# Relaying the opening of a fused QK-norm attention and leaky-ReLU MLP kernel on one core

## The chip, the cores and the metric

The kernel runs on one core of a Trainium2 chip. A core has four compute engines, each with a queue of its own that it works through in order: TensorE (PE, matmuls and transposes), VectorE (DVE), ScalarE (ACT) and GpSimd (POOL). SyncE (SP) issues most of the transfers; POOL and ACT can issue some too. Engines wait for each other only through semaphores. The metric is the device time in microseconds of one execution.

## The reference

```python
def _attn_ref(q, k, v, g_q, g_k):          # q, k, v: 8 x 12 x 448 x 64
    def rmsnorm(x, g):
        rms = np.sqrt(np.mean(x * x, axis=-1, keepdims=True) + 1e-06)
        return x / rms * g
    q_n, k_n = (rmsnorm(q, g_q), rmsnorm(k, g_k))
    scores = 1.0 / np.sqrt(64) * np.matmul(q_n, k_n.transpose(0, 1, 3, 2))
    attn = np.exp(scores - np.max(scores, axis=-1, keepdims=True))
    attn = attn / (np.sum(attn, axis=-1, keepdims=True) + 1e-09)
    return np.matmul(attn, v)

# x: the heads side by side, 3584 tokens x 768
h = x @ w_in                               # 768 x 2048
out = np.maximum(0.01 * h, h) @ w_out      # 2048 x 768
```

## The kernel before

**Units.** The attention is worked through in 24 units: one batch and four of its twelve heads each (NQ = 3 units to a batch). A unit goes through these steps, each in a function of its own:

- `load` (L104) brings q and k of the unit with two transfers on SP into the tiles rq and rk (three buffers each); `load_v` (L110) brings v on POOL's queue into one of four tiles.
- The squares of q and k: `prep_sq` (L129) on ACT or `prep_sqp` (L133) on POOL. Their sums along each row, `prep_ssq` (L140), on DVE. One over the root, `prep_rinv` (L145), on ACT, as the exponential of minus half a logarithm. The product of the data with it, `prep_norm` (L150), on DVE: this is called norm(u) here. It reads two tensors in SBUF. The squares on POOL read two as well.
- The transposes: on PE in units 0 to 5 (`prep_tr`, L158, with a copy out of PSUM by DVE or ACT), by a transfer (`prep_trd`, L165) later.
- `qk` (L185) computes the scores transposed, seven steps t of 128 keys by 448 queries for four heads, into one of two PSUM slots. `ex` (L192) exponentiates a step on ACT, with a shift that is the same for the whole unit. The shift comes from the maximum of step 0: `shift_max` (L208, DVE) reduces along the rows and builds a diagonal, `shift_mm` (L226) spreads it over the partitions by a matmul with ones on PE and takes the maximum on DVE. For units 1 and 2, `score0` (L203) computes step 0 into two banks outside the slots.
- `zsum_slot` (L255) or `zcol` (L261) sums the exponentials by matmuls with ones, `pv` (L319) multiplies with v, `zinv` (L308) inverts the sums on ACT, `xmul` (L329) multiplies, which gives three pieces of x per batch.

**The two matmuls of the MLP** are cut into items of about a microsecond of PE time, which wait in a list (`queue`, filled by `push`, L499, when a batch is complete). `fill` (L534) runs after each quarter d of a unit and takes as many items from the list as its rate asks for; between the items it emits jobs of the coming units (`jobs`: norms, sums of squares, loads). The second matmul of two row blocks at a time is done with seven products in place of eight (`seven`, L422), with sums of blocks of the weights (`weight_sum`, L398, into the tile tw) and of the activations (s1 to s4, into the tile sa). The evacuations of the banks ma, mb, mc and md by DVE or ACT are not emitted at once, but put on a list (`pend`, through `later`, L419), which the next item empties (`flush`, L372) before its own matmuls. At the end of `fill`, L552 empties that list, and then L553 emits the jobs that are left over.

**The opening** is written out by hand (L576 to L746). Units 0, 1 and 2 are prepared there, and PE is given filler matmuls (`warm`, L572) in places where it would have nothing to do. `gate(u)` (L242) copies a single element of norm(u) on POOL, so that whatever comes after it in POOL's queue waits until that norm is done. The squares of units 1 to 8 are on POOL. `close(u)` (L642) ends unit u: sums, the first two exponentials of the next unit around them, products, and the inverse. The order in which the functions are called is the order in each engine's queue.

The weights come through POOL's queue: `load_w_in` (L87) in two halves of four transfers, `load_w_out` (L92) in two transfers.

The four names that the prediction uses most: rinv is the result of `prep_rinv`; sq are the squares; dg the diagonal; eb the finished shift.

Of the kernel before, what the change touches and what calls it, by code (L numbers as in the profile page):

```python
# [18 lines left out]
def kernel(  # L19
# [11 lines left out]
    nc = tc.nc  # L31
# [23 lines left out]
    def aux(shape, dtype, name):  # L55
        return psum.tile(shape, dtype, tag="aux", bufs=4, name=name)
# [53 lines left out]
    def load_v(u):  # L110
        nc.gpsimd.dma_start(vts[u % NV].rearrange("p a t d -> p a (t d)"), rows(v, u))  # L111
# [21 lines left out]
    def prep_sqp(u, tis=BOTH):  # L133
        for ti in tis:
            nc.gpsimd.tensor_tensor(buf(u, f"sq{ti}"), raw[u][ti], raw[u][ti], op=ALU.mult)
# [236 lines left out]
    def flush():  # L372
        while pend:
            pend.pop(0)()
# [159 lines left out]
    def fill(u, d, jobs):  # L534
        total = sum(c for c, _ in queue)
        left = WD[d] + 3.0
        uu, dd = u, d
        while True:
            dd += 1
            if dd == 4:  # L540
                uu, dd = uu + 1, 0
            if uu == NU or (fed(uu, dd) and (u > 3 or uu > 3)):
                break
            left += WD[dd]
        debt[0] += total * WD[d] / left
        while queue and debt[0] >= queue[0][0] * 0.5:
            c, fn = queue.pop(0)
            fn()
            debt[0] -= c
            if jobs:  # L550
                jobs.pop(0)()
        flush()  # L552
        for job in jobs:  # L553
            job()

    def vcopy(dst, src, scaled=False):
        if scaled:
# [18 lines left out]
    with tc.manual_schedule():  # L576
# [19 lines left out]
        nc.vector.tensor_copy(gcol, gps[:, 0:1])  # L596
        prep_ssq(0, ALL, (1,))
        prep_rinv(0, (1,))
        prep_sqp(1, (0,))
        load_v(0)  # L600
        load_v(1)
        prep_norm(0, CA, (0,))
        prep_norm(0, CB, (0,))
        prep_tr(0, 0, ((CA, acopy), (CB, acopy)))
        prep_norm(0, K0, (1,))
        tpk = aux([P, NS, P], FP16, "tp")

        def trk(c, copy):
            for x in range(*c):
                nc.tensor.transpose(tpk[:, x, :], buf(0, "n16")[:, 1, x].rearrange("p a d -> p (a d)"), ident16)  # L610
            copy(buf(0, "qkT")[:, 1, c[0]:c[1]], tpk[:, c[0]:c[1]])

        trk(K0, vcopy)
        prep_norm(0, K1, (1,))
        qk(0, STEPS[0])
        shift_max(0)
        trk(K1, acopy)
        load(3)
        prep_sqp(1, (1,))
        gate(0)  # L620
        load_w_in(0, 1024)
        prep_sqp(2)
        shift_bank(0)
        warm(12, st[0]["pb"])
        shift_mm(0)
        load_v(2)
        prep_ssq(1, ALL, (0,))

        def feed(u):
            load(u + 4)  # L630
# [8 lines left out]
            zsum(u, t0, t1)  # L639
            pv(u, t0, t1)  # L640

        def close(u):  # L642
            n = u + 1
            zsum_slot(u)
            ex(n)
            qk(n, (1,))
            pv(u)
            zinv(u)

        ex(0)  # L650
        prep_ssq(1, ALL, (1,))
        prep_rinv(1)
        prep_norm(1)
        prep_ssq(2)
        feed(0)
        load_w_in(1024, 1024)
        wb = aux([P, 512], FP32, "warm")
        qk(0, (1,))
        ex(0)
        warm(16, wb)  # L660
        qk(0, (2,))
        ex(0)
        warm(12, wb)
        qk(0, (3,))
        ex(0)
        warm(6, wb)
        qk(0, (4,))
        ex(0)
        trn(1, 0, vcopy)
        trn(1, 1, acopy)  # L670
        qk(0, (5,))
        ex(0)
        qk(0, (6,))
        ex(0)
        prep_rinv(2)
        score0(1)
        shift_max(1)
        shift_bank(1)
        warm(20, st[1]["pb"])
        shift_mm(1)  # L680
        close(0)

        prep_norm(2)
        prep_ssq(3)
        ex(1)
        feed(1)
        for f in range(2):
            load_w_out(8 * f, 8)
# [8 lines left out]
        ex(1)  # L697
        qk(1, (5,))
        ex(1)
        prep_rinv(3)  # L700
        score0(2)
        shift_max(2)
        qk(1, (6,))
# [1 line left out]
        shift_bank(2)  # L705
        warm(12, st[2]["pb"])
        shift_mm(2)
        close(1)

        prep_norm(3)  # L710
        ex(2)
        feed(2)
        qk(2, (2,))
        ex(2)
# [33 lines left out]
        for u in range(3, NU):  # L748
            for d in range(4):
                if d > 0 or u > 3:  # L750
                    qk(u, STEPS[d])
                    if d == 0:
                        shift_max(u)
                        if narrow(u - 1):
                            pv_slot(u - 1)
                            zcol(u - 1)
                            shift_mm(u)
                            pv_out(u - 1)
                            zcol_sum(u - 1)
                        else:  # L760
                            zsum_slot(u - 1)
                            pv(u - 1)
                            shift_mm(u)
                            zinv(u - 1)
                    ex(u)
                jobs = []

                def job(fn, *args):
                    jobs.append(lambda: fn(*args))

                if d == 0:
                    if u == 3:
                        prep_norm(4)
                        gate(4)
                    elif narrow(u - 1):
                        job(zcol_inv, u - 1)
                    else:
                        xmul(u - 1)
                    if u + 4 < NU:
                        job(load, u + 4)  # L780
                    if u + 3 < NU:
                        load_v(u + 3)
                    if u < 6:
                        prep_sqp(u + 3)
                if d == 1 and narrow(u - 1) and not 5 <= u < 8:
                    xmul_pool(u - 1)
                if fed(u, d) and u > 3:
                    push(u // NQ - 1)
                if (u, d) in ((3, 1), (4, 0)):
                    for ti in range(2):  # L790
                        prep_tr(u + 1, ti, VV)
                if d == 1 and 5 <= u < NU - 1:
                    job(prep_g, u + 1)
                if u + 2 < NU:
                    if d == 1:
                        for ti in range(2):
                            job(prep_ssq, u + 2, ALL, (ti,))
                    if d == 2:
                        job(prep_rinv, u + 2)
                        for ti in range(2):  # L800
                            job(prep_norm, u + 2, ALL, (ti,))
                        if u > 3:
                            job(prep_trd, u + 2)
                if d == 1 and 4 <= u < 8:
                    job(weight_sum, u - 4, 0)
                if d == 0 and 5 <= u < 9:
                    job(weight_sum, u - 5, 1)
                if d == 2 and 5 <= u < 8:
                    job(xmul_sb, u - 1)
                if d == 3 and 6 <= u < NU - 3:  # L810
                    for ti in range(2):
                        job(prep_sq, u + 3, ALL, (ti,))
                fill(u, d, jobs)
# [36 lines left out]
```

## Time and profile before

| | |
|---|---|
| median of 4 runs | 431.1 us (430.36 to 431.43) |
| the profiled execution | 431.01 us, span 429.2 us |
| PE busy | 409.5 us (95%) |
| ACT busy | 306.4 us (71%) |
| DVE busy | 270.9 us (63%) |
| POOL busy | 87.2 us (20%) |
| mean granted TensorE clock | 0.987 |
| first sum or product of the MLP on PE | 46.47 us |

The span is from the first to the last instruction of the profiled execution; its own time is 1.8 us longer. A share of busy time over the whole span is an average over stages with different limits, so the table of busy times by stage says more. In the timelines each line has the start, the time that the group of instructions covers, the engine, the line of the kernel, the operation and the tiles (result, arrow, sources), the shape, the count, and in brackets the idle time before it with what ended it. Ends of neighbouring instructions overlap by about 0.1 us, since the next begins while the last drains.

### The profile page before, as it was taken

What the parts mean: (1) busy time and instruction counts of PE and PEld (TensorE: products, weight loads), DVE (VectorE), ACT (ScalarE), POOL (GpSimd) and SP (SyncE); (2) the same over time, 40 slices, a digit from 0 to 9 for tenths busy, and PEclk for the clock granted to TensorE, in tenths of its full rate; (3) what the DMA queues carried; (4) which work ended last, traced back from release to release, by engine and by line L of the source; (5) the groups of instructions that cost most, each with busy time, mean ns of one, the idle gap of its engine ahead of it and who ended that gap; (6) DMA issues with size and microseconds to landing.
All of it is one profiled execution on the core that took longest, in us unless ns stands there. A gap on an engine that the chain in (4) does not pass through costs nothing.

```text
span 429.2 us, 8844 instructions
## 1 busy us (share of the span) xinstructions
PE 409.5 (95%) x3645; PEld 211.0 (49%) x3645; DVE 270.9 (63%) x434; ACT 306.4 (71%) x466; POOL 87.2 (20%) x77
## 2 busy tenths in 40 slices
PE   7687999999999999999999999999999999999996
PEld 6454444444444544455445544455445544455563
DVE  5887656888669865487359864587449840541162
ACT  5569888757986779967986789967986767643400
POOL 2985323300002102111102102111101101110000
PEclk9869999999999999999999999999999999999999
DMA  7999992789656896578665797478672460212013
GB/s 265 219 243 248 240 270 52 121 182 221 168 105 116 190 214 159 143 135 193 170 111 130 190 192 171 130 141 188 169 110 44 118 150 10 44 38 73 2 45 103
DMA packets 66476, 62.37 MB, mean 145 GB/s; under 512 B 35716, under 2 KB 61572, under 8 KB 66436
## 3 DMA queue, kind: packets, MB, share of 16 engines
q1 hardware_dynamic: 55840, 49.62, 46.4%
q0 software_dynamic: 10272, 11.80, 18.0%
q8 instruction: 28, 0.46, 0.4%
q10 hardware_dynamic: 324, 0.39, 0.3%
q14 instruction: 12, 0.10, 0.1%
HBM read 45.61 MB, written 11.01 MB: 132 GB/s over the span
## 4 chain that ended last, share of the span: by engine, by line
PE 66%; ACT 18%; DVE 9%; issue 2%; DMA 1%; SPq 0%; ACTq 0%; DVEq 0%
PE hps L347 23%; ACT et L201 9%; PE md L427 7%; PE mc L427 7%; PE sT L182 6%; PE ma L427 6%; PE sT L326 5%; ACT gt L341 4%; PE op L387 3%; DVE n L154 3%; PE zc L269 3%; PE mb L427 2%; ACT x L281 1%; PE sT L252 1%; ACT zs L292 1%
## 5 line engine op out<-in xcount | busy, mean ns | idle before, releaser
L201 ACT ACTIVATE et<-sT,eb 128x896 f16<-128x896 f32 x166 | 158.3, 1003 | 15.7 <-PE sT L182 13.3
L347 PE MATMUL hps<-xt,win 128*128 128x448 f16 x756 | 151.1, 353 | 0.2 <-DVE xt L335 0.2
L347 PEld LDWEIGHTS <-win 128*128 128x128 f16 x756 | 70.6, 98 | 71.5 <-issue 10.2
L341 ACT ACTIVATE gt<-hps 128x448 f16<-128x448 f32 x126 | 65.6, 540 | 19.4 <-PE hps L347 18.7
L306 POOL TENSOR_TENSOR xt<-x,rz 128x896 f16<-128x896 f32 x16 | 33.5, 2092 | 149.6 <-DMA rz<-zs 57.0
L154 DVE TENSOR_TENSOR n<-rq,rinv 128x896 f16<-128x896 f32 (+2 forms) x25 | 28.5, 1142 | 47.5 <-ACT rinv L148 44.1
L182 PE MATMUL sT<-qkT 64*64 64x448 f16 x664 | 52.5, 367 | 5.6 <-ACT et L201 4.8
L142 DVE TENSOR_REDUCE ssq<-sq 128x14 f32<-128x896 f32 (+2 forms) x49 | 50.3, 1057 | 0.7 <-ACT sq L131 0.7
L427 PEld LDWEIGHTS <-sa 128*128 128x128 f16 x352 | 32.8, 98 | 26.3 <-issue 6.1
L281 ACT COPY x<-sT 128x896 f32<-128x896 f32 x19 | 17.2, 906 | 37.8 <-DVE sT L232 37.8
L111 POOL DMA_DIRECT2D vt<-in_v_dram x24 | 18.2, 758 | 112.6 <-PE sT L326 105.1
L219 DVE TENSOR_REDUCE sT<-sT 128x1 f32<-128x896 f32 x22 | 24.1, 1094 | 18.1 <-PE sT L182 18.1
L182 PEld LDWEIGHTS <-qkT 64*64 64x64 f16 x672 | 15.8, 105 | 39.6 <-issue 36.1
L427 PEld LDWEIGHTS <-gt 128*128 128x128 f16 x264 | 25.2, 98 | 19.0 <-issue 2.9
L387 PE MATMUL op<-wout,gt 128*128 128x384 f16 x192 | 34.1, 327 | 0.0
L427 PE MATMUL ma<-wout,gt 128*128 128x384 f16 x176 | 32.2, 326 | 0.4
L326 PE MATMUL sT<-et,vt 64*64 64x448 f16 x532 | 28.5, 349 | 0.3
L154 DVE TENSOR_TENSOR n<-rk,rinv 128x896 f16<-128x896 f32 (+2 forms) x25 | 28.2, 1128 | 0.0
L408 DVE TENSOR_TENSOR sa<-gt 128x512 f16<-128x512 f16 (+1 forms) x15 | 8.1, 542 | 30.3 <-ACT gt L341 30.3
L326 PEld LDWEIGHTS <-vt 64*64 64x64 f16 x672 | 20.4, 107 | 10.9 <-issue 1.1
L387 PEld LDWEIGHTS <-gt 128*128 128x128 f16 x192 | 17.7, 98 | 14.0 <-issue 3.2
L453 ACT COPY ost<-ma 128x384 f32<-128x384 f32 x11 | 5.3, 478 | 23.7 <-PE ma L427 23.7
(87 smaller groups left out, 444.6 us busy)
## 6 DMA issues: line engine op xcount, KB each, us to landing
rq<-in_q_dram SPq DMA_DIRECT2D x24, 448.0 KB, 5.0
rk<-in_k_dram SPq DMA_DIRECT2D x24, 448.0 KB, 5.9
out_dram<-ost SPq DMA_DIRECT2D x52, 192.0 KB, 4.1
rz<-zs SPq DMA_DIRECT2D x38, 224.0 KB, 3.3
vt<-in_v_dram POOLq DMA_DIRECT2D x24, 224.0 KB, 5.1
win<-in_moe_w_in_dram POOLq DMA_DIRECT2D x8, 384.0 KB, 8.6
wout<-in_moe_w_out_dram POOLq DMA_DIRECT2D x2, 1536.0 KB, 22.7
out_dram<-ost SPq DMA_DIRECT2D x4, 96.0 KB, 2.1
```

Source lines behind the costliest of these rows:

```text
L142: nc.vector.tensor_reduce(buf(u, "ssq")[:, ti, :, c[0]:c[1]], buf(u, f"sq{ti}")[:, :, c[0]:c[1]], axis=AXL.X, op=ALU.add)
L154: nc.vector.tensor_tensor(buf(u, "n16")[:, ti, c[0]:c[1]].rearrange("p s a d -> p a s d"), src[:, :, c[0]:c[1]], buf(u, "rinv")[:, ti, :, ...
L182: nc.tensor.matmul(banks[a][64 * r:64 * r + 64, 0:S].rearrange("p (t x) -> p t x", t=NS), kT(u, r, a, t), qT(u, r, a), start=True, stop=True)
L201: nc.scalar.activation(s["et"][:, t], sT[:, :, 0:S], AF.Exp, bias=s["eb"], scale=1.0)
L219: nc.vector.tensor_reduce(s["spare"][:, 511:512], sT[:, :, 0:S], axis=AXL.XY, op=ALU.max)
L281: nc.scalar.copy(s["x32"], s["pslot"][:, :, 0:S])
L306: eng.tensor_tensor(xts[b][:, g], s["x32"], s["rz"], op=ALU.mult)
L326: nc.tensor.matmul(s["pv"][r][64 * a:64 * a + 64, 0:S], vts[u % NV][64 * r:64 * r + 64, a, t], s["et"][64 * r:64 * r + 64, t, a], start=(t ...
L341: nc.scalar.activation(dst, src, AF.Prelu, bias=0.0, scale=1.0, alpha=0.01)
L347: nc.tensor.matmul(hps[:, 0:S], win16[:, kt // 2, kt % 2, ts(ft, P)], xt[:, kt // 2, kt % 2], start=(kt == 0), stop=(kt == KT - 1))
L387: nc.tensor.matmul(op2[:, 0:HC], gt[:, ft, ds(col(t), P)], wout16[:, ft, ds(HC * half, HC)], start=(ft == 0), stop=(ft == FT - 1))
L427: nc.tensor.matmul(bank[:, 0:HC], a[:, f], b[:, f], start=(first and f == 0), stop=(f == HF - 1), skip_group_check=not first)
```

## The change

The opening is written in another order, and two things in the loop are moved.

- POOL's queue now begins with `gate(0)`. After it come the v of unit 0, the squares of unit 2, the first half of w_in, the v of units 1 and 2, `gate(1)`, the second half of w_in, and the squares of unit 3. The squares of unit 1 are computed on ACT instead, between the copies of unit 0's transposes.
- The transposes of unit 0 are done by a function `tr`, which takes a PSUM tile of its own for each chunk of q. Norm K1 is emitted before K0's copy.
- Unit 1's rinv is computed in two parts among the exponentials of unit 0; its norm in three pieces; its transposes, scores of step 0 and maximum follow after the fifth exponential of unit 0, and the matmul that finishes its shift after the last one. The copies of its transposes go to ACT (q) and DVE (k).
- `close` is dissolved: after the shift of unit u + 1 come the sums of squares of unit u + 2, two exponentials of unit u + 1, then the sums and the products of unit u, the rinv of unit u + 2, the inverse of unit u, and norm(u + 2). This is done at the end of units 0 and 1.
- The fillers between the exponentials change in number and place (6 before the matmul of the shift of unit 0 instead of 12, then 12 and 16 instead of 16, 12, 6 and 20).
- In `fill`, the left-over jobs are emitted first, and then the pending evacuations.
- The second half of each weight sum is emitted in the last quarter of the same unit, instead of the first quarter of the next.

```diff
@@ -549,9 +549,9 @@
             debt[0] -= c
             if jobs:
                 jobs.pop(0)()
-        flush()
         for job in jobs:
             job()
+        flush()
 
     def vcopy(dst, src, scaled=False):
         if scaled:
@@ -596,35 +596,39 @@
         nc.vector.tensor_copy(gcol, gps[:, 0:1])
         prep_ssq(0, ALL, (1,))
         prep_rinv(0, (1,))
-        prep_sqp(1, (0,))
-        load_v(0)
-        load_v(1)
         prep_norm(0, CA, (0,))
         prep_norm(0, CB, (0,))
-        prep_tr(0, 0, ((CA, acopy), (CB, acopy)))
         prep_norm(0, K0, (1,))
-        tpk = aux([P, NS, P], FP16, "tp")
-
-        def trk(c, copy):
-            for x in range(*c):
-                nc.tensor.transpose(tpk[:, x, :], buf(0, "n16")[:, 1, x].rearrange("p a d -> p (a d)"), ident16)
-            copy(buf(0, "qkT")[:, 1, c[0]:c[1]], tpk[:, c[0]:c[1]])
-
-        trk(K0, vcopy)
         prep_norm(0, K1, (1,))
+
+        def tr(u, ti, chunks, tp=None):
+            if tp is None:
+                tp = aux([P, NS, P], FP16, "tp")
+            for c, copy in chunks:
+                for x in range(*c):
+                    nc.tensor.transpose(tp[:, x, :], buf(u, "n16")[:, ti, x].rearrange("p a d -> p (a d)"), ident16)
+                copy(buf(u, "qkT")[:, ti, c[0]:c[1]], tp[:, c[0]:c[1]], ti == 0)
+            return tp
+
+        tr(0, 0, ((CA, acopy),))
+        tr(0, 0, ((CB, acopy),))
+        tpk = tr(0, 1, ((K0, vcopy),))
+        prep_sq(1, ALL, (0,))
         qk(0, STEPS[0])
         shift_max(0)
-        trk(K1, acopy)
+        tr(0, 1, ((K1, acopy),), tpk)
+        prep_sq(1, ALL, (1,))
         load(3)
-        prep_sqp(1, (1,))
         gate(0)
+        load_v(0)
+        prep_sqp(2)
         load_w_in(0, 1024)
-        prep_sqp(2)
+        load_v(1)
+        load_v(2)
         shift_bank(0)
-        warm(12, st[0]["pb"])
+        warm(6, st[0]["pb"])
         shift_mm(0)
-        load_v(2)
-        prep_ssq(1, ALL, (0,))
+        prep_ssq(1)
 
         def feed(u):
             load(u + 4)
@@ -639,50 +643,48 @@
             zsum(u, t0, t1)
             pv(u, t0, t1)
 
-        def close(u):
-            n = u + 1
-            zsum_slot(u)
-            ex(n)
-            qk(n, (1,))
-            pv(u)
-            zinv(u)
-
         ex(0)
-        prep_ssq(1, ALL, (1,))
-        prep_rinv(1)
-        prep_norm(1)
-        prep_ssq(2)
-        feed(0)
-        load_w_in(1024, 1024)
-        wb = aux([P, 512], FP32, "warm")
+        prep_rinv(1, (0,))
         qk(0, (1,))
         ex(0)
-        warm(16, wb)
+        prep_rinv(1, (1,))
+        prep_norm(1, ALL, (0,))
+        prep_norm(1, K0, (1,))
+        prep_norm(1, K1, (1,))
+        load(4)
+        gate(1)
+        load_w_in(1024, 1024)
+        prep_sqp(3)
+        load_v(3)
+        wb = aux([P, 512], FP32, "warm")
+        warm(12, wb)
         qk(0, (2,))
         ex(0)
-        warm(12, wb)
+        warm(16, wb)
         qk(0, (3,))
+        tr(1, 0, ((ALL, acopy),))
+        tpk = tr(1, 1, ((K0, vcopy),))
         ex(0)
-        warm(6, wb)
         qk(0, (4,))
         ex(0)
-        trn(1, 0, vcopy)
-        trn(1, 1, acopy)
+        tr(1, 1, ((K1, vcopy),), tpk)
+        score0(1)
+        shift_max(1)
         qk(0, (5,))
         ex(0)
         qk(0, (6,))
         ex(0)
+        shift_bank(1)
+        shift_mm(1)
+        prep_ssq(2)
+        ex(1)
+        qk(1, (1,))
+        ex(1)
+        zsum_slot(0)
+        pv(0)
         prep_rinv(2)
-        score0(1)
-        shift_max(1)
-        shift_bank(1)
-        warm(20, st[1]["pb"])
-        shift_mm(1)
-        close(0)
-
+        zinv(0)
         prep_norm(2)
-        prep_ssq(3)
-        ex(1)
         feed(1)
         for f in range(2):
             load_w_out(8 * f, 8)
@@ -697,7 +699,6 @@
         ex(1)
         qk(1, (5,))
         ex(1)
-        prep_rinv(3)
         score0(2)
         shift_max(2)
         qk(1, (6,))
@@ -705,10 +706,16 @@
         shift_bank(2)
         warm(12, st[2]["pb"])
         shift_mm(2)
-        close(1)
+        prep_ssq(3)
+        ex(2)
+        qk(2, (1,))
+        ex(2)
+        zsum_slot(1)
+        pv(1)
+        prep_rinv(3)
+        zinv(1)
 
         prep_norm(3)
-        ex(2)
         feed(2)
         qk(2, (2,))
         ex(2)
@@ -801,10 +808,8 @@
                             job(prep_norm, u + 2, ALL, (ti,))
                         if u > 3:
                             job(prep_trd, u + 2)
-                if d == 1 and 4 <= u < 8:
-                    job(weight_sum, u - 4, 0)
-                if d == 0 and 5 <= u < 9:
-                    job(weight_sum, u - 5, 1)
+                if d in (1, 3) and 4 <= u < 8:
+                    job(weight_sum, u - 4, d // 2)
                 if d == 2 and 5 <= u < 8:
                     job(xmul_sb, u - 1)
                 if d == 3 and 6 <= u < NU - 3:
```

## The prediction

> **What bounds the kernel now.** I read the stage table first: busy time per engine in four stretches, then the granted TensorE clock, the DMA share and GB/s.
>
> ```profile
> core 0: us, PE busy (x) PEld busy (x) DVE busy (x) ACT busy (x) POOL busy (x), PEclk, DMA share, GB/s
> 15.00:30.00 15.00, 10.79 (x133) 6.94 (x134) 12.84 (x15) 9.05 (x15) 13.11 (x16) 0.77 1.13 231
> 30.00:46.50 16.50, 13.13 (x226) 7.94 (x219) 13.34 (x21) 16.24 (x23) 9.97 (x10) 1.00 1.12 247
> 46.50:100.00 53.50, 50.68 (x474) 24.81 (x470) 40.03 (x57) 40.49 (x62) 13.29 (x11) 1.00 0.81 169
> 100.00:388.00 288.00, 286.64 (x2503) 140.93 (x2496) 183.28 (x295) 223.72 (x339) 44.01 (x30) 1.00 0.62 137
> ```
>
> From 46.5 us on TensorE is full (286.64 of 288.00), so the end moves one for one with two things: when that stretch starts, and any new PE wait in it. From 30 to 46.5 ScalarE is full (16.24 of 16.50): the exponentials set the pace. Before 30 neither is; DVE and POOL are (12.84 and 13.11 of 15.00). The list of waits says how little PE waits after 100 us:
>
> ```profile
> PE sT L231 <- DVE dg L221: 0.7, 3, 0.2
> ```
>
> The timelines of POOL and DVE (start, duration) show what fills 16 to 22:
>
> ```profile
> 16.40 1.69 POOL L135 TENSOR_TENSOR sq<-rq 128x896 f32<-128x896 f32 x1
> ...
> 16.67 2.38 DVE L154 TENSOR_TENSOR n<-rq,rinv 128x896 f16<-128x896 f32 x1 [0.70 <-issue]
> ...
> 18.04 2.54 POOL L135 TENSOR_TENSOR sq<-rk 128x896 f32<-128x896 f32 x1
> ...
> 18.98 2.56 DVE L154 TENSOR_TENSOR n<-rk,rinv 128x896 f16<-128x896 f32 x1
> ...
> 27.59 1.09 DVE L154 TENSOR_TENSOR n<-rq,rinv 128x896 f16<-128x896 f32 x1
> ```
>
> A norm takes 1.09 alone. Beside a square on POOL the two take turns: norm q ends 1.0 after the first square, the second square ends 1.6 after norm q, norm k 1.0 after that. So norm(1) ends at 21.54 instead of about 18.7. The transposes of unit 1 and ScalarE (idle 2.18 at 20.2 and 2.21 at 25.5) wait for it.
>
> **The opening, part by part.** I walk the new order with the old durations; ex(u,t) is exponential t of unit u (0.91 start to start).
>
> 1. Shift of unit 0. Norm K1, blocked 9.80 to 11.35 by POOL's square of unit 1, now runs 8.6 to 9.5; K0's copy ends 9.62; CB's transposes no longer wait for CA's copy, so scores start at 9.75 (was 10.23). Maximum 1.08, diagonal 0.29, matmul 0.23, 0.30 and 0.16: shift ready at 12.6 (was 13.98; six fewer fillers stand before the matmul). The two squares of unit 1 on ScalarE (0.95 each, k data landed 9.97) fit behind the copies, done 12.4. Gain 1.35.
> 2. Norm(1). Sums of squares to 13.65 and 14.6, rinv q to 14.2, ex(0,1), rinv k to 15.5; norm q 14.6 to 15.65, K0, K1 to 16.75. POOL is then issuing w_in, which the norms are priced as not disturbing: at 27.1 and 27.7 the same issues ran beside a norm of 1.09 and took 0.63 to 0.68. Was 21.54. The split rinv costs 0.52 more of ScalarE.
> 3. Shift of unit 1. q copy on ScalarE 16.35 to 17.35, K1 copy on DVE to 17.9, scores 0.4, two maxima 1.16, then 1.3 to the shift: 20.9, just as ex(0,6) ends (12.6 + 7 x 0.91 + two rinv 1.07 + copy 1.0 = 21.0). So ex(1,0) starts at 21.0, was 27.73. The sums and products of unit 0 move behind ex(1,1); their 28 matmuls of sums (1.5) are done at 22.5 and ScalarE wants them at 23.6, so the move is free unless PE is over 1 us late.
> 4. Norm(2) wants 23.6 (two sums of squares after the shift, rinv after ex(1,1)). What is late next is POOL. Its queue: gate(0) 9.6, v0, squares(2) 11.1 to 14.45 (data landed 11.08 and 12.27), w_in 4 x 0.63 to 17.0, v1, v2 to 18.5, gate(1), w_in again, squares(3). The instruction list has the third and fourth of these w_in wait until the first two w_in have landed (eight completion counters in turn). Those landed 5.9 and 7.1 us after issue; from 14.4 and 15.1 that is 20.3 and 22.2, v1 no longer ahead but load(4) beside them 3 us sooner: I take 21.7 for the second. Squares(3) then start near 22 and collide with norm(2), which ends 26.6 to 28.4 (by whose turn it is) rather than 25.6. I take 27.1. Behind gate(0), now at the head of POOL's queue, the first w_in goes from 13.84 to 14.4 and v0 from 10.48 to 9.8; their first users come at 22 (products of unit 0) and about 42, so this costs nothing. On SP only load(k, 3) (11.42 to 9.6) and load(4) (19.1 and 21.6 to 15.7 and 16.9) move, still in the same order and each behind its norm.
> 5. Unit 2's shift comes 4.75 after norm(2) ends: copies 1.27, xmul 1.07, maxima 1.16, then to the exponential (33.71 to 37.27 in the trace is xmul onward, 3.56). ex(2,0): 31.8, bounds 30.3 to 33.15; was 37.27.
> 6. Unit 2 itself gets longer: rinv(3) (0.57) now inside, and scores(2,3) stand behind transposes of norm(3), which starts later (after rinv(3)): ex(2,6) ends 9.6 after ex(2,0), was 8.46. So 41.4 instead of 45.73.
>
> Gain of the opening 4.3. Bounds: 5.85 without any collision; 3.0 with the worst turn, 2.5 with a clock drop. The clock: in equal 3.4 us stretches of before, those at full clock with PE busy 36% and 34% were followed by one at 0.50, those with 71% and 87% were not; the new stretches from 8.2 to 21.8 are about 65 to 75% busy by this walk. A drop costs 28 matmuls 2.31 instead of 1.52 twice (1.6), some 0.5 of which ScalarE would feel. I take none, as 65% is nearer to 71.
>
> The Trainium skill, "TensorE: Matmul & The Clock Gate", Part 1, says the clock drops after an idle window; the rows show it dropping after windows a third busy. By the page no new window could drop it and the term is 0 for certain; by the rows it is 0 to 0.5.
>
> [...]
>
> **The steady stretch.** Nothing is added; DVE work is put elsewhere.
>
> - The pending add of the md bank now follows norm k. It occurs five times (149.41, 195.68, 245.57, 292.13, 342.04). The timeline of the first, DVE and PE:
>
> ```profile
> 148.41 1.09 DVE L154 TENSOR_TENSOR n<-rq,rinv 128x896 f16<-128x896 f32 x1 [0.31 <-ACT rinv L148]
> ...
> 149.23 1.47 PE L427 MATMUL mc<-wout,sa 128*128 128x384 f16 x8
> 149.41 0.55 DVE L434 TENSOR_TENSOR ost<-md,ost 128x384 f32<-128x384 f32 x1
> 149.88 1.08 DVE L154 TENSOR_TENSOR n<-rk,rinv 128x896 f16<-128x896 f32 x1
> ...
> 150.54 1.46 PE L427 MATMUL md<-tw,gt 128*128 128x384 f16 x8
> ```
>
>   PE adds into md again at 150.54, so it must wait for that add: now 148.41 + 2 x 1.005 (norms back to back) + 0.55 + 0.05 (the usual step from DVE to PE, 91.40 to 91.45) = 151.02. PE loses 0.48. The third place is spared (next md matmuls at 249.58). 4 x 0.48 = 1.9; bounds 0 and 5 x 1.01.
> - At 225.00 and 321.45 sa's sums wait for ScalarE with a sum of squares (1.0) behind them, ahead of the ma copy; PE's second ma matmuls start 0.29 late (227.39, where mb's start of 225.79 + 8 x 0.163 is 227.10). Now that sum of squares fills the wait. Gain 2 x 0.29 = 0.6.
> - Second halves of the weight sums (0.95, one 1.67 beside a POOL square) move from the start of a unit to the end of the one before, ahead of its maximum. End of unit 4: DVE has 0.22 spare, dg ends 77.98 instead of 77.42, PE is ready at 77.9: 0.1. Unit 5: one moved out at 81.25, one in, DVE full throughout: 0. Unit 6: 0.56 spare plus the one moved out: 0. Unit 7: DVE is full from 115.47 to the maximum and PE already waits 0.23 for it at 121.41: the whole 0.95. Sum 1.05; bounds 0 and 4 x 0.95.
>
> Loss 1.9 - 0.6 + 1.05 = 2.35. No transfer is made larger. Loads ask up to 5 us sooner of queues that are full until 62; the weights for the sum at 68.5 landed at 52.1, so 12 us cover that.
>
> **Sum.** 431.01 (the profiled execution; span 429.2 and 1.8 around it; 0.1 under the median of 431.1) - 4.3 + 2.35 = 429.06; against the median **429.2 us**.
>
> **The rivals.**
> - POOL is early or takes the kind turn, norm(2) ends by 25.6 (for it: v1 is out of w_in's way; against: load(4) is in it): 431.1 - 5.85 + 2.35 = 427.6; with PE slack half as bad, 426.5.
> - The opening loses more: worst turn and a clock drop, 431.1 - 2.5 + 2.35 = 431.0. No change.
> - Slower: DVE, 63% busy overall but full around the maxima, becomes the bound: each moved instruction delays PE by its whole length, 5 x 1.01 + 4 x 0.95 = 8.85, giving 431.1 - 4.3 + 8.85 - 0.6 = 435.0. It decides once the steady loss passes 4.3 + 0.9 = 5.2. Against: 1.4 us of PE slack at units 4 to 6 as read above.
> - Slower by a wait that replaces one: rinv(3) sits in ScalarE's queue ahead of zinv(1) and needs squares(3). If the second w_in lands after 28.8 each us costs one; at 17.9 after issue (the slowest v) 33.0, so +4.2: 433.4. In before it landed at 21.6.
>
> **How the numbers follow.** Forecast 0.46 (own range 428.1 to 430.2), kind POOL 0.20, opening lost 0.17, full DVE 0.12, late w_in 0.05. The measurement tells about 0.2% (0.9 us) from no change: faster 0.66, same 0.17, slower 0.17. Leaving out under 0.1 at either end: 426.8 to 432.2.
>
> **What would show it.** Norm(1) at 1.09 with no POOL square beside it; ex(1,0) near 21, ex(2,0) near 31.8; norm(2) stretched past 1.09 beside squares(3); ScalarE with under 2 us idle from 13 to 41; four md waits of 0.48 and one of about 1.1 before the shift matmul near 118. Wrong if ex(2,0) is outside 30.3 to 33.2, or if PE's waits after 100 stay at 0.7 or pass 5.

## The result and the profile after

The changed kernel takes 432.0 us (median of 43 runs, 431.08 to 434.06) against 431.12 us for the kernel before (64 runs beside it, 430.29 to 432.76): ratio 1.0024, 95% interval 1.0018 to 1.0030. It is 0.9 us slower, where 1.9 us faster was forecast. The profiled execution of after took 432.57 us, span 430.8 us, so it lies 0.6 us above its own median; before's lay 0.1 us below.

The table of busy times by stage, of after (stretch and length; busy time and count for PE, PEld, DVE, ACT, POOL; granted TensorE clock; DMA share; GB/s):

```profile
15.00:30.00 15.00, 10.37 (x125) 6.17 (x123) 12.96 (x16) 11.31 (x17) 11.32 (x17) 0.84 0.97 195
30.00:46.50 16.50, 13.30 (x198) 7.30 (x195) 13.62 (x22) 14.17 (x20) 9.86 (x9) 0.94 1.14 247
46.50:100.00 53.50, 50.63 (x470) 24.73 (x468) 40.59 (x57) 40.20 (x62) 13.29 (x11) 1.00 0.85 181
100.00:388.00 288.00, 284.74 (x2485) 139.80 (x2483) 182.32 (x292) 223.28 (x339) 44.01 (x30) 1.00 0.63 137
```

Three things differ from before. From 15 to 30 ScalarE does 2.26 us more (11.31 instead of 9.05): the opening did get ahead. From 30 to 46.5 it does 2.07 us less (14.17 instead of 16.24): most of the lead was given back there. And after 100 PE is 1.90 us less busy (284.74 instead of 286.64): the new waits of the loop. The list of waits of PE after 100 us names them (total, times, longest):

```profile
PE sT L231 <- DVE dg L221: 1.6, 3, 1.1
PE md L427 <- DVE ost L434: 1.3, 4, 0.3
```

The place where the lead was lost shows in the timelines of POOL, DVE and ACT of after, 13 to 36 us:

```profile
13.75 1.68 POOL L135 TENSOR_TENSOR sq<-rk 128x896 f32<-128x896 f32 x1 [0.64 <-DVE ssq L142]
15.38 2.54 POOL L90 DMA_DIRECT2D win<-in_moe_w_in_dram  x4
...
20.97 0.63 POOL L90 DMA_DIRECT2D win<-in_moe_w_in_dram  x1 [0.25 <-DMA win<-in_moe_w_in_dram]
...
23.61 0.63 POOL L90 DMA_DIRECT2D win<-in_moe_w_in_dram  x1 [2.02 <-DMA win<-in_moe_w_in_dram]
24.13 4.41 DVE L154 TENSOR_TENSOR n<-rq,rinv 128x896 f16<-128x896 f32 x1 [1.04 <-issue]
24.26 1.69 POOL L135 TENSOR_TENSOR sq<-rq 128x896 f32<-128x896 f32 x1
25.90 1.68 POOL L135 TENSOR_TENSOR sq<-rk 128x896 f32<-128x896 f32 x1
...
28.46 1.08 DVE L154 TENSOR_TENSOR n<-rk,rinv 128x896 f16<-128x896 f32 x1
...
30.08 1.01 ACT L201 ACTIVATE et<-sT,eb 128x896 f16<-128x896 f32 x1 [2.62 <-PE sT L182]
...
35.03 1.16 ACT L199 ACTIVATE et<-s,eb 128x448 f16<-128x448 f32 x2 [0.77 <-DVE eb L240]
```

POOL stands 2.02 us before the last transfer of w_in, until an earlier one of the same weights has landed. So the squares of unit 3 start at 24.26, within 0.13 us of the moment when norm(2) starts, and they are issued back to back. Norm q takes 4.41 us in place of 1.09: it is through only 1.0 us after the second square. PE has no transposed data of unit 2, ScalarE idles 2.62 us, and ex(2,0) starts at 35.03.

The loop's two losses, in the timelines of DVE and PE of after, stand as the prediction described them. Near 120 the moved weight sum is ahead of the maximum, and near 150 the md addition is behind norm k:

```profile
118.60 0.95 DVE L402 TENSOR_TENSOR tw<-wout,tw 128x1536 f16<-128x1536 f16 x1
121.60 0.22 PE L231 MATMUL sT<-dg,onesp 128*128 128x64 f16 x2 [1.10 <-DVE dg L221]
...
149.42 1.47 PE L427 MATMUL mc<-wout,sa 128*128 128x384 f16 x8
149.60 1.08 DVE L154 TENSOR_TENSOR n<-rk,rinv 128x896 f16<-128x896 f32 x1
150.60 0.55 DVE L434 TENSOR_TENSOR ost<-md,ost 128x384 f32<-128x384 f32 x1
...
151.21 1.46 PE L427 MATMUL md<-tw,gt 128*128 128x384 f16 x8 [0.32 <-DVE ost L434]
```

From mc to md PE needs 1.79 us (149.42 to 151.21) instead of the 1.31 us of before (149.23 to 150.54): 0.48 us, at four places.

### The profile page after: what moved, and what is told of

Read it like the earlier page. It is cut to its first block, busy times and chain, and to the rows that moved or that the text cites. A ratio compares the mean times of both kernels' runs of the same rounds, so it can differ in the third digit from the quotient of the medians.

```text
span 430.8 us, 8784 instructions
## 1 busy us (share of the span) xinstructions
PE 409.2 (95%) x3613; PEld 208.8 (48%) x3613; DVE 272.8 (63%) x436; ACT 308.7 (72%) x470; POOL 83.1 (19%) x75
## 4 chain that ended last, share of the span: by engine, by line
PE 64%; ACT 16%; DVE 14%; issue 4%; DMA 1%; SPq 0%; DVEq 0%; ACTq 0%
PE hps L347 25%; ACT et L201 8%; PE ma L427 7%; PE md L427 6%; PE sT L182 6%; DVE n L154 5%; PE sT L326 4%; PE op L387 4%; PE mc L427 4%; PE mb L427 3%; ACT gt L341 3%; PE zc L269 3%; DVE sT L219 1%; DVE ssq L142 1%; DMA rk<-in_k_dram 1%
## 5 line engine op out<-in xcount | busy, mean ns | idle before, releaser
L154 DVE TENSOR_TENSOR n<-rq,rinv 128x896 f16<-128x896 f32 (+2 forms) x25 | 30.9, 1241 | 50.5 <-ACT rinv L148 46.0
L427 PEld LDWEIGHTS <-gt 128*128 128x128 f16 x264 | 25.2, 98 | 20.3 <-issue 4.3
L154 DVE TENSOR_TENSOR n<-rk,rinv 128x896 f16<-128x896 f32 (+2 forms) x26 | 26.1, 1010 | 0.0
L453 ACT COPY ost<-ma 128x384 f32<-128x384 f32 x11 | 5.3, 478 | 23.6 <-PE ma L427 23.6
```

What stands on the lines that cost most here:

```text
L154: nc.vector.tensor_tensor(buf(u, "n16")[:, ti, c[0]:c[1]].rearrange("p s a d -> p a s d"), src[:, :, c[0]:c[1]], buf(u, "rinv")[:, ti, :, ...
L427: nc.tensor.matmul(bank[:, 0:HC], a[:, f], b[:, f], start=(first and f == 0), stop=(f == HF - 1), skip_group_check=not first)
```

## The experiments

Two landmarks in each trace split a run into opening and loop. M is the start of the last two matmuls of batch 0's first row block in the first MLP matmul, the ones that wait for the last `xmul` of the batch (49.09 in before). From there PE is full. The loop is counted from M to the start of the last md group on PE (423.68 in before). All are from the one profiled execution of each kernel; the medians stand beside them, with before's of the same chip.

| kernel | norm(2) ends | ex(2,0) | M | M to last md | median | before beside it |
|---|---|---|---|---|---|---|
| before | 29.68 | 37.27 | 49.09 | 374.59 | 431.12 | |
| after | 29.54 | 35.03 | 48.43 | 376.79 | 432.00 | 431.12 |
| new loop alone | 29.59 | 37.39 | 49.21 | 376.95 | 433.18 | 431.06 |
| new opening alone | 29.09 | 34.43 | 47.83 | 374.60 | 429.82 | 431.06 |
| jobs before evacuations alone | 29.65 | 36.62 | 48.44 | 375.90 | 432.79 | 430.62 |
| weight sums alone | 29.72 | 37.10 | 48.92 | 375.60 | 431.82 | 430.62 |
| after, squares first | 26.19 | 32.86 | 46.26 | 376.81 | 429.24 | 431.06 |
| after, squares apart | 29.69 | 34.50 | 47.94 | 376.74 | 432.05 | 431.06 |
| after, fillers | 29.22 | 34.50 | 47.90 | 376.75 | 432.51 | 431.01 |
| after, v of units 1 and 2 moved | 26.02 | 30.79 | 49.99 | 376.76 | 434.20 | 431.01 |
| after, v of unit 1 moved | 26.97 | 31.74 | 45.13 | 376.72 | 429.44 | 431.01 |
| opening, squares first, old loop | 26.46 | 31.23 | 44.62 | 374.59 | 426.87 | 430.62 |
| the same and fillers | 26.14 | 30.90 | 44.30 | 374.54 | 426.28 | 430.62 |
| v of 1 and 2 moved, fillers, old loop | 27.73 | 32.74 | 49.80 | 374.61 | 431.99 | 431.01 |

The column of the loop takes only four values (374.6, 375.6, 375.9 and 376.8, to within 0.15 us), whatever the opening does. So whatever an edit wins or loses ahead of M arrives whole at the end, and opening and loop can be read apart.

**Opening and loop apart.** First the loop's two edits on before:

```diff
-        flush()
         for job in jobs:
             job()
+        flush()
...
-                if d == 1 and 4 <= u < 8:
-                    job(weight_sum, u - 4, 0)
-                if d == 0 and 5 <= u < 9:
-                    job(weight_sum, u - 5, 1)
+                if d in (1, 3) and 4 <= u < 8:
+                    job(weight_sum, u - 4, d // 2)
```

> The opening of before with the loop of after (jobs ahead of the pending evacuations, second halves of the weight sums a quarter earlier). If the loop costs what PE's waits in the trace of after show, 4 x 0.48 for the md add, 0.9 for the shift of unit 8, less 2 x 0.3 for the ma copies, the time is 431.1 + 2.3 = 433.4. If the loop were neutral and the whole loss came out of the opening: 431.1.

Measured: 433.18 us (432.70 to 433.79), ratio 1.0052 (1.0034 to 1.0070), +2.1 us on the medians; the loop is 2.36 us longer.

Then the rest of the change with these two edits taken back:

```diff
@@ fill, of after
+        flush()
         for job in jobs:
             job()
-        flush()
@@ jobs, of after
-                if d in (1, 3) and 4 <= u < 8:
-                    job(weight_sum, u - 4, d // 2)
+                if d == 1 and 4 <= u < 8:
+                    job(weight_sum, u - 4, 0)
+                if d == 0 and 5 <= u < 9:
+                    job(weight_sum, u - 5, 1)
```

> The opening of after with the loop of before. If opening and loop add up: the last part of the first MLP sum starts 0.66 sooner (49.09 to 48.43), so 431.1 - 0.7 = 430.4. If the new opening only looked faster and moved its loss later (a transfer or a buffer that is late after 48 us), 431.1 or more.

Measured: 429.82 us (429.50 to 430.35), ratio 0.9973 (0.9963 to 0.9984), 1.2 us faster, and a loop of 374.60, before's to 0.01. The parts add up: -1.24 + 2.12 = +0.88, and the whole change measured +0.88 (that they agree to the hundredth is luck: the interval of each part is 0.9 us wide or more). The loop's loss is what was forecast; the opening's gain is short of its 4.3 by 3.

**The loop's two edits apart.** Only the order of jobs and evacuations (first hunk above):

> The kernel before with one edit: the jobs of a group stand ahead of the pending evacuations. By the terms of the prediction, 4 x 0.48 us for the gated products that start one md addition later, less 2 x 0.29 us for the two places where the ma copies come earlier: +1.3 us on the kernel before (431.1), so 432.4. Rival: these shifts at the seams are taken up again by TensorE's queue behind them and cost nothing: 431.1. Second rival: the loop's loss lies in the weight sums, this edit takes less than 0.5 us of it.

Only the weight sums (second hunk above):

> The kernel before with one edit: the weight sums go from groups (1, u - 4) and (0, u - 5) to groups 1 and 3 of unit u. Together with the order of jobs and evacuations the loop cost 2.12 us. By the prediction this part costs 1.05 us, in the shift's diagonal of unit 7 that stands behind a weight sum on VectorE: 432.1, with one wait of TensorE for that diagonal near 1 us where before had 0.23 us. Rival: in before's order of jobs and evacuations the weight sum falls at another moment and hides: 431.1.

Measured: 432.79 us (ratio 1.0049, 1.0037 to 1.0061) and 431.82 us (1.0022, 1.0013 to 1.0031). The waits of PE after 100 us separate cleanly. Jobs ahead of evacuations:

```profile
PE md L427 <- DVE ost L434: 1.3, 4, 0.3
PE sT L231 <- DVE dg L221: 0.7, 3, 0.2
```

Weight sums moved:

```profile
PE sT L231 <- DVE dg L221: 1.6, 3, 1.1
```

The loop is longer by 1.31 us with the first (forecast 1.3) and by 1.01 us with the second (forecast 1.05). The weight sums' median agrees (+1.2). That of the other edit stands at +2.2, beyond the 1.31 of its trace. The opening is the same there, yet M wanders from 48.44 to 49.21 in the four executions that have before's opening. The times of this edit begin and end 1.4 us above before's (431.71 to 433.17 against 430.26 to 431.74), so I read the rest of its median as the part of that spread in which its six runs fell; this is argued, not shown. It fits that the medians of the two single edits sum to 3.4 us, while both edits in one kernel cost 2.1.

**Is it the squares of unit 3 that keep norm(2) back?** They go ahead of the second half of w_in:

```diff
         gate(1)
-        load_w_in(1024, 1024)
         prep_sqp(3)
+        load_w_in(1024, 1024)
         load_v(3)
```

> After, with the squares of unit 3 on POOL ahead of the second half of w_in instead of behind it. If norm(2) was late because it waited for those squares: they run at 19.5 to 21.2 and 22.1 to 23.8 and are done when norm(2) is wanted at 24.1; norm(2) takes 1.1 + 1.1, ex(2,0) goes from 35.0 to 31 to 32, and the time from 432.0 to about 428.7. If the half clock of PE from 21.9 to 25.3 and 28.7 to 32.1 (sums 2.74, products 2.07) is what delays unit 2, ex(2,0) stays above 34 and the time within 0.8 of 432.0.

Measured: 429.24 us (428.20 to 431.65), ratio 0.9958 (0.9940 to 0.9976): 2.8 us below after by this one line. The norm's two halves take 1.09 and 1.08 us and end at 26.19, beside the issues of w_in (timelines of POOL and DVE):

```profile
23.76 2.55 POOL L90 DMA_DIRECT2D win<-in_moe_w_in_dram  x4
24.10 1.09 DVE L154 TENSOR_TENSOR n<-rq,rinv 128x896 f16<-128x896 f32 x1 [1.04 <-POOL sq L135]
25.11 1.08 DVE L154 TENSOR_TENSOR n<-rk,rinv 128x896 f16<-128x896 f32 x1
```

But ex(2,0) comes at 32.86, not 31 to 32. The stage rows of this run show the next limit:

```profile
18.47:21.88 3.41, 1.80 (x17) 0.76 (x20) 3.00 (x8) 3.41 (x5) 2.69 (x4) 0.78 1.08 216
21.88:25.29 3.41, 3.41 (x40) 2.06 (x36) 2.37 (x4) 2.87 (x6) 3.15 (x4) 0.50 1.11 264
25.29:28.71 3.42, 3.42 (x46) 1.87 (x39) 1.58 (x2) 2.34 (x4) 3.42 (x5) 0.72 1.13 239
```

TensorE is at half clock from about 21 to 27, where the sums and products of unit 0 stand (28 matmuls of sums take 2.83 us). In after this had been hidden behind the late norm. The ten executions of this kernel follow their clock: 428.2 to 428.65 us at a mean granted clock of 0.994 and up, 429.2 to 430.4 at 0.988 to 0.992, 431.65 at 0.984.

The same squares, left behind w_in, but with the v of unit 3 between them:

```diff
         load_w_in(1024, 1024)
-        prep_sqp(3)
+        prep_sqp(3, (0,))
         load_v(3)
+        prep_sqp(3, (1,))
```

> After, with the transfer of v of unit 3 (0.77 of POOL) issued between the two squares of unit 3. If a norm that waits loses its turn to a second square because that one stands directly behind the first, the gap lets it in: norm q takes 2.8 instead of 4.41, norm k then waits for the second square (2.6 instead of 1.08), and the two end near 29.5 as before, so the time stays within 0.8 of 432.0. If norm q waits for something other than the squares, it stays at 4.4.

Measured: 432.05 us, in a single execution and so without an interval. The timelines of POOL and DVE:

```profile
24.07 1.70 POOL L135 TENSOR_TENSOR sq<-rq 128x896 f32<-128x896 f32 x1
24.07 2.65 DVE L154 TENSOR_TENSOR n<-rq,rinv 128x896 f16<-128x896 f32 x1 [1.01 <-issue]
26.25 0.77 POOL L111 DMA_DIRECT2D vt<-in_v_dram  x1 [0.49 <-DMA win<-in_moe_w_in_dram]
26.64 3.05 DVE L154 TENSOR_TENSOR n<-rk,rinv 128x896 f16<-128x896 f32 x1
27.04 1.69 POOL L135 TENSOR_TENSOR sq<-rk 128x896 f32<-128x896 f32 x1
```

With a gap behind the first square norm q gets in (2.65 instead of 4.41), and then norm k has to wait for the second. The sum is the same, and so is the time. What costs is that the two squares meet the norm at all; the order in which they take turns decides nothing here.

**Why are the squares so late?** The third and fourth w_in of the second half waited 0.25 and 2.02 us for a landing. Seven other transfers of POOL's queue lie between each and the one that it waited for, the first and the second w_in of the first half: each waited for the eighth before it. The wait of 0.49 us before the v of unit 3 in the run with the squares apart (26.25) is of the same kind; its eighth before is the third w_in of the first half. One load fewer in between should shift that wait to an earlier landing:

```diff
         load_v(0)
+        load_v(1)
         prep_sqp(2)
         load_w_in(0, 1024)
-        load_v(1)
         load_v(2)
```

> After with one load moved on GpSimd's queue: that of v of unit 1 directly behind that of unit 0; that of unit 2 stays where it was. By the reading of the landing waits (a transfer of GpSimd's queue waits for the landing of the eighth before it), the last transfer of w_in's second half then waits for the first landing of the first half, near 21, and no longer for the second, near 23.6. So the squares of unit 3 start near 21.6, as step 4 of the prediction took it, the norm of unit 2 meets the end of the second square and ends near 26 to 27, the first exponential of unit 2 starts near 31 to 32 us (after: 35.03), v of unit 2 is in time, and the time is 428.5 to 429.5 us, where the prediction had it. Rival: the landing of v of unit 1, not of w_in, or the descriptors set the squares' place: no change from 432.0.

Measured: 429.44 us (428.54 to 430.38), ratio 0.9966 (0.9954 to 0.9978). The timelines of POOL, DVE and ACT:

```profile
21.04 0.63 POOL L90 DMA_DIRECT2D win<-in_moe_w_in_dram  x1 [0.62 <-DMA win<-in_moe_w_in_dram]
21.68 1.69 POOL L135 TENSOR_TENSOR sq<-rq 128x896 f32<-128x896 f32 x1
23.33 1.68 POOL L135 TENSOR_TENSOR sq<-rk 128x896 f32<-128x896 f32 x1
...
23.94 2.03 DVE L154 TENSOR_TENSOR n<-rq,rinv 128x896 f16<-128x896 f32 x1 [1.04 <-POOL sq L135]
...
31.74 1.16 ACT L199 ACTIVATE et<-s,eb 128x448 f16<-128x448 f32 x2 [0.98 <-DVE eb L240]
```

This is the opening that the prediction had priced: squares from 21.7 (near 22), norm(2) done at 26.97 (27.1), ex(2,0) at 31.74 (31.8). Between after and this run the start of the squares differs by 2.58 us and the end of norm(2) by 2.57. Its profiled execution took 429.2 us, the number that was forecast; that it agrees so closely is partly luck, since M (45.13) came 0.3 us later than a gain of 4.3 gives and the loop was 0.2 us shorter than forecast.

Two loads fewer in between, with v of unit 2 put behind the squares of unit 3:

```diff
         load_v(0)
+        load_v(1)
         prep_sqp(2)
         load_w_in(0, 1024)
-        load_v(1)
-        load_v(2)
...
         prep_sqp(3)
+        load_v(2)
         load_v(3)
```

> After with two loads of v moved on GpSimd's queue: that of unit 1 stands directly behind that of unit 0, that of unit 2 behind the squares of unit 3. The second half of w_in still stands ahead of the squares of unit 3. In after its third and fourth transfer waited 0.25 and 2.02 us for a landing of the first half; eight transfers lie between such a pair. With two loads fewer between, those waits should fall on the two early loads of v and be gone: w_in issued from near 18.0 to 20.6, squares of unit 3 from 20.6 to about 24.0, norm of unit 2 undisturbed (1.1 us each), and the time near 429.2, as with the squares issued first. Rival: the queue waits for its own transfers whatever stands between; then the squares stay near 24 us and the time at 432.0.

(Seven transfers lie between such a pair; the one waited for is the eighth before.)

Measured: 434.20 us (433.62 to 434.85), ratio 1.0072 (1.0052 to 1.0092). The chain behaved as expected up to unit 2: w_in was issued from 17.83 to 20.3 without a wait, the norm's halves took 1.09 and 1.08, ex(2,0) came at 30.79, 4.2 us before after's. Then PE stood, in its timeline:

```profile
42.35 1.33 PE L326 MATMUL pv<-et,vt 64*64 64x448 f16 x12 [4.16 <-DMA vt<-in_v_dram]
```

The v of unit 2, issued near 24 behind all of w_in, landed at 42.3, and its products waited 4.16 us. The time that I named (429.2) missed by 5 us because I followed the two transfers that I had freed and not the one that I had put back. The same opening with fillers and before's loop met the same wait (3.1 us):

> After's opening with the two loads of v moved and the fillers, and before's steady loop. If the landing wait, the half clock and the loop are the three losses: 426.3, as the run with the early squares, fillers and old loop, or up to 0.5 us less, since w_in stands earlier. Rival: v of unit 2 or 1 now lands late, and the products of unit 1 or 2 wait for it: above 427.

Measured: 431.99 us (ratio 1.0023, 1.0012 to 1.0035), M at 49.80: the rival's side. Its profiled execution also had a stretch of TensorE clock at 0.59 from 18.47 to 21.88 in spite of the fillers.

**Is the half clock a loss of its own?** Fillers alone, on after:

```diff
-        warm(6, st[0]["pb"])
+        warm(12, st[0]["pb"])
...
         shift_max(1)
+        shift_bank(1)
         qk(0, (5,))
         ex(0)
+        warm(8, st[1]["pb"])
         qk(0, (6,))
         ex(0)
-        shift_bank(1)
+        warm(8, st[1]["pb"])
         shift_mm(1)
```

> After with the fillers on TensorE alone (12 instead of 6 behind shift 0, twice 8 between the last score tiles of unit 0), nothing moved on GpSimd and the new loop kept. If the norm of unit 2 is what ends the opening, TensorE's half clock lies beside its two lost turns and the fillers gain little: 431.3 to 432.0, with the first exponential of unit 2 near 34.4 us and the norm of q still above 4 us. Rival: the half clock is a loss of its own that adds to the late norm: 430.8 or less, and that exponential below 33.7 us.

Measured: 432.51 us (431.99 to 433.26), ratio 1.0032 (1.0020 to 1.0044), which overlaps after's own: nothing gained, and 0.5 us above the range that I had named. The clock was full up to 28.7 and the 28 matmuls of sums took 1.52 us, but norm q of unit 2 still took 4.33 us and ex(2,0) came at 34.50. The stage rows show that the late norm then takes the clock with it:

```profile
25.29:28.71 3.42, 0.44 (x7) 0.39 (x7) 3.42 (x2) 1.20 (x2) 2.67 (x3) 1.00 1.14 238
28.71:32.12 3.41, 3.09 (x30) 1.42 (x27) 2.97 (x6) 2.34 (x3) 1.81 (x2) 0.50 1.18 214
```

PE has 0.44 us of work in the 3.4 us in which it waits for the norm, and runs the next ones at 0.50. So as long as the norm is late, the fillers are spent for nothing.

**A version that beats both.** After's opening with the squares of unit 3 first, and before's loop:

> After's opening with the squares of unit 3 issued on GpSimd ahead of the second half of w_in, and before's steady loop (jobs behind evacuations, weight sums where they were). If the parts add up: 431.1 - 1.24 (the opening alone) - 2.8 (the squares first, measured on after) = 427.1 us. Rival: both edits reach the same slack further on, and part of the 2.8 us had been the loop's own waits: 428 or more.

Measured: 426.87 us (425.92 to 427.98), ratio 0.9911 (0.9897 to 0.9925). The sum of parts had given 427.1: they add up again.

The same with the fillers:

> As the run that joins the relaid opening with the early squares of unit 3 and the old loop, with fillers on TensorE: 12 instead of 6 behind shift 0, and twice 8 between the last score tiles of unit 0, so that the stretches of some 3.4 us that were 46 to 58% busy come above 64%. If the half clock in 21.9 to 28.7 us costs: no clock of 0.50 in 18.5 to 28.7, the sums and the products of unit 0 take near 1.5 us each instead of 2.8 us, the first exponential of unit 2 starts 1 to 1.5 us earlier, and the time is 0.7 to 1.5 us below that run. Rival: the chain runs through VectorE's norms and ScalarE there, and the fillers only stand ahead of real products: within 0.3 us of that run, or above it.

Measured: 426.28 us (426.02 to 427.09), ratio 0.9900 (0.9887 to 0.9913), 4.3 us faster than the kernel before. The timelines of DVE, PE and ACT of this run, the lines that answer to those of after at 24 to 36 us:

```profile
21.61 1.52 PE L252 MATMUL sT<-et,ones 64*64 64x448 f16 x28 [0.49 <-ACT et L201]
...
24.05 1.09 DVE L154 TENSOR_TENSOR n<-rq,rinv 128x896 f16<-128x896 f32 x1 [0.73 <-issue]
25.06 1.08 DVE L154 TENSOR_TENSOR n<-rk,rinv 128x896 f16<-128x896 f32 x1
...
30.90 1.16 ACT L199 ACTIVATE et<-s,eb 128x448 f16<-128x448 f32 x2 [0.66 <-DVE eb L240]
```

Norm(2) runs at its bare length, ex(2,0) starts 4.13 us before after's, and no stretch from 8 to 35 us is below full clock. Against the run without fillers the medians differ by 0.6 us and the two spreads overlap, so a gain of the fillers is likely here, not shown: the profiled execution without them had full clock from 18.5 on as well (ex(2,0) at 31.23).

## Why the prediction was wrong

The steady stretch was right in sum and in parts: 2.35 us forecast, 2.20 in after's trace; 1.3 and 1.31 for the order of jobs and evacuations, 1.05 and 1.01 for the weight sums. The opening was to gain 4.3 us at M and gained 0.66 in the profiled execution (1.2 on the medians of the opening alone). ex(2,0), at 35.03, lies outside the 30.3 to 33.2 that the prediction had named as the sign of its being wrong. The missing 3.64 us sit in three steps:

- **Step 4, norm(2)'s end: 2.44 us (29.54 instead of 27.1).** "I take 21.7 for the second" landing of w_in was the term that failed: it landed near 23.6. One half of the 1.9 us is an issue that came 0.9 us late: 0.64 us because the square of k of unit 2 waited for DVE to finish with the tile of squares that it reuses (POOL's timeline, 13.75), a wait that the walk left out, and 0.3 because the square of q started that much later, when its data landed. The other half is a landing 7.6 us after issue where 6.6 had been taken. "Near 22" for the squares also left out some 0.3 us of the last issue itself (21.7 + 0.63). Moving one load gave the assumed landing back, and the forecast with it (429.44 us). The bounds of 26.6 to 28.4 had only the turns in them, with the squares at 22; the landing had no bound of its own, although it moved the squares one for one.
- **Step 5, from norm(2) to ex(2,0): 0.74 us (5.49 instead of 4.75).** That is TensorE's half clock, which the sum took as 0. In four runs with full clock over this stretch it is 4.76 to 4.77, and in the three with a clock of 0.50 or 0.51 from 28.7 to 32.1 (after, the new opening alone, after with fillers) 5.28 to 5.49. The bound of 0.5 is not far off in size, but that is luck: it was for a drop at the sums of unit 0. That drop came too (2.74 us for the 28 matmuls) and lay beside the late norm; the one that cost came after it, at 0.51 from 28.7 to 32.1, when PE had stood waiting for norm(2) (1.23 us busy in the 3.4 us before).
- **Step 6, the length of unit 2: 0.43 us.** From ex(2,0) to ex(2,6)'s end after takes 10.03 us instead of 9.6, and 10.02 to 10.07 in every other run with the new opening in which v of unit 2 was in time. Two exponentials wait 0.49 us each for their scores, besides rinv(3): the scores of the first stand behind the transposes of norm(3) in PE's queue, those of the second behind sums and products of unit 2. The walk had counted about one such wait.

Together 3.61 of the 3.64 us. These sizes are of one execution, 0.6 us above its median; in the run with the new opening alone the same steps missed by 1.99, 0.59 and 0.44, which is 3.02 of the 3.04 us that it lacks. Steps 1 and 3 held: ex(0,0) at 12.72 against 12.6, ex(1,0) at 21.50 against 21.0. In step 2 norm(1) ended at 17.45 instead of 16.75, beside that late square of unit 2; ScalarE was busy with exponentials meanwhile, and only 0.5 us came through.

Of the rivals, "the opening loses more" came nearest (431.0 with the worst turn and a clock drop). The one on the slower side had the right cause and the wrong path: it let a late w_in act through rinv(3) only, from 28.8 us on, while it acted through the squares' turn with the norm from 21.7 on. Of the full DVE no more was seen than the sum had: the loop cost 2.20 us, not the 5.2 from which that rival would have decided.

Step 2 had priced the norms as not disturbing the issues of w_in. That held: the run with squares first issued four transfers of w_in beside both halves of norm(2) in 2.55 us, some 0.63 each, as without a norm (2.54 for the four from 13.84 in before).

The Trainium skill, "SBUF — State Buffer", "two separate sides", has an exclusive lock between a VectorE operation with two inputs in SBUF and a GpSimd operation that reads SBUF: the one that starts first has the shared ports for its whole length, and the other blocks fully. That the loser blocks fully fits the rows here: a norm that waited ends 0.95 to 0.97 us after the square it waited for. That the first to start wins does not, by the starts in the rows: norm q of after begins at 24.13, before the square at 24.26, and norm k of the run with the squares apart at 26.64, before the square at 27.04, and both waited.

## What to carry to other kernels

When a step moves in a queue that also issues transfers, list every wait that the queue meets on the way (a tile still being read, a transfer's landing), give each its own bound, and carry it to the instructions behind it: a landing that nobody needs for its data can still set the time of the compute behind it. Check what a moved load meets at its own first user. And a cost that looks free because it lies beside a longer wait (here the half clock) is the next limit once that wait is gone, so it belongs into the sum of the better version.

## What was not expected of the hardware

- **Who gets the next turn.** In before and in two runs with its opening, norm(1) got in between two squares that stood back to back (2.38, 2.76 and 2.22 us for norm q). In after and in two runs with its opening and order, norm(2) waited for both (4.41, 4.21, 4.33). The moment of arrival doesn't tell them apart: 0.11 us before the first square in one of the former, 0.13 before it in one of the latter. This stays open.
- **A norm that started ahead of a square still waited for it.** In the run with the squares apart norm k, at 26.64, had 0.4 us until the square of k, in which POOL was issuing v, and was not through until that square was. The issue itself does not explain it: in the run with v of two units moved and fillers, norm k too began while v was being issued, and took its bare length. This stays open.

```profile
25.64 1.09 DVE L154 TENSOR_TENSOR n<-rq,rinv 128x896 f16<-128x896 f32 x1 [0.70 <-issue]
25.65 1.49 POOL L111 DMA_DIRECT2D vt<-in_v_dram  x2
26.65 1.08 DVE L154 TENSOR_TENSOR n<-rk,rinv 128x896 f16<-128x896 f32 x1
```

- **The clock has no simple threshold here.** The Trainium skill, "TensorE: Matmul & The Clock Gate", Part 1, has the clock drop after an idle window of about 3.4 us. The stretch with 0.44 us of work agrees. But in after's trace the stretch from 8.23 to 11.64 with PE busy 1.99 us (58%) was followed by 0.51. With v of two units moved and fillers, even one with 2.26 us (66%) was followed by 0.59. And at the same place the run with two loads moved (first two rows) and that with one load moved (last two) had the same 54%, with opposite outcomes:

```profile
8.23:11.64 3.41, 1.83 (x24) 1.17 (x23) 2.81 (x6) 3.03 (x5) 2.00 (x4) 1.00 0.95 316
11.64:15.05 3.41, 2.74 (x41) 2.04 (x40) 3.07 (x6) 3.13 (x6) 2.92 (x2) 1.00 1.06 236
...
8.23:11.64 3.41, 1.84 (x24) 1.18 (x23) 2.81 (x6) 3.02 (x5) 1.99 (x4) 1.00 0.93 312
11.64:15.05 3.41, 3.31 (x29) 2.21 (x29) 3.07 (x6) 3.12 (x6) 2.92 (x2) 0.54 1.01 214
```

So a share of busy time of 65%, which the prediction took as enough, is not safe, and the shares of stretches counted from the span's start don't say when the drop comes.
